# Hedgehog linear attention and softmax attention behind one gate: more score tiles on VectorE, feature sums and products on GpSimd, a written-out order

## The chip, the cores and the metric

The kernel runs on one core of a Trainium2 chip. The metric is device time in microseconds, the median of several runs. A core has five engines with a queue each: TensorE (PE, matrix products; PEld is its weight load), VectorE (DVE), ScalarE (ACT), GpSimd (POOL) and SyncE (SP, which here issues DMAs). They wait for one another by semaphores. TensorE writes to PSUM, 128 partitions by eight banks of 512 f32; here VectorE and ScalarE read PSUM, GpSimd works on SBUF alone.

## What is computed

One input `x` (1 x 2048 x 512, bf16) goes through two attention blocks of 32 heads with 16 features each, and a sigmoid gate mixes them:

```python
g = _sigmoid((x * gate_w).sum(-1, keepdims=True))
a = _A_ref(x, A_wqkv, A_w_phi, A_wo)      # linear attention, Hedgehog features
b = _B_ref(x, B_wqkv, B_wo)               # softmax attention
return g * a + (1 - g) * b
```

Block A maps q and k of each head by a 16 x 16 matrix, takes `softmax(p)` and `softmax(-p)` as 32 features, and computes `phi_q (phi_k^T v)` over `phi_q (sum of phi_k) + 1e-6`. Block B is plain softmax attention over 2048 keys: 32 heads x 2048 x 2048 exponentials. Both end in a 512 x 512 projection.

## The kernel before

**Block B** makes up most of the work. Its scores are cut into 32 blocks b of four heads i and 512 queries, each with 16 key tiles: 2048 tiles (b, i, kt) of 128 keys x 512 queries. A tile is one matmul with 32 rows of contraction (`qk_mm`, L1299 to L1303); four tiles of different heads can sit in the four row groups of the array. Values come by a second matmul into 32 columns (`pv_mm`, L1408 to L1415), accumulated in one bank, `psO`, for a whole block; a column of ones beside V gives the denominator.

The exponential of a tile is made in one of two ways:

- On **ScalarE**: a *slot* of two tiles in two PSUM banks, one `activation(Exp)` over 128 x 1024 (`add_exp`, L1392), into the ring `Ebuf`. Banks 0, 1 and 2, 3 alternate. 1304 tiles go this way, in 652 slots.
- On **VectorE**: `tensor_scalar` adds a constant and writes int16, whose bits read as bf16 are an approximate power of two (L1378; two tiles in one instruction, a *pair*, L1368). A *group* of up to four tiles of one block fills a buffer `t`. GpSimd then makes two copies shifted by constants with a 64-bit integer add (`shifted`, L1347 to L1358; L1354): `s` from `t`, then `m` over `s`. The value product is done for all three (`add_pvd`, L1416 to L1441): terms "t" and "s" in one piece of PE work, "m" in another, a round of up to four column tiles each. The counts of these tiles by block are `DN` (L31), 744 in all, in 195 groups. The scores of such a tile go to one of three shared banks, `MISC`, which also serve all other products. `PHASES` (L32) says which parts of SBUF serve as `t` and `s` from which block on.

When a block is done, `psO` is copied (L1507), the denominators go out to DRAM and come back transposed, are inverted, go out and come back broadcast as `Rb` (SP's moves in `add_norm`), and one product (L1523) scales two heads' rows into `oT`.

**Block A** is spread between as *fills* (`fill`, `drain`): a fill takes a bank, runs its matmuls, and a drain empties it. `columns` (L1060) splits a product with 128 output rows into four column tiles. For each 128 rows, `phi` (L1658) projects (L1062), takes exp of +p and -p on ScalarE (L1669), and for each two steps sums each head's 16 features. The sum is a product by the identity, 16 matmuls of 64 columns a step (L1676). For k, the reciprocal goes to `stat` (L1691) and scales V (`va_fill`, L1650; a small copy on GpSimd, L1655). For q, the ratio of the two sums (L1682, L1684, L1686) scales the second half of the features (`scaled_q`, L1703), and SP writes them to DRAM to be read transposed. `kv_half` and `kfinal` (L1732, L1735) build the masked state, `z_rest` and `q_rest` apply it.

**V** of block B for head rows 0 and 1 comes by `v_fill` (L1153), for rows 2 and 3 together by `v_pair` (L1166), 64 matmuls of 128 x 128 weights and 256 columns. `out_tile` and its kin do the projections; their sums meet in one bank.

**Order.** `Plan.add` notes each piece of work with engine, estimated duration, priority and what it reads and writes. `Plan.layout` (L538) lays all out in time on the five engines by a list schedule. It also puts in *fillers*: products with a zero weight tile (`zero_mm`, L1401 to L1406; L1403), where its estimate of TensorE's activity in the last 3.41 us (`WINDOW`, `ACTIVE`) falls under a limit, as pieces of their own ("idle") or ahead of a value product (`extra`). Pieces marked `lock` are kept from running on VectorE and GpSimd at once. `Plan.settle` (L780) then applies the table `MOVES`: changed places in each queue, pairs, `locks` (a GpSimd piece that waits for a given VectorE piece), banks, and fillers that are dropped. `Plan.emit` writes the queues; each engine runs its own strictly in that order, and waits where a piece needs another engine's.

Of the kernel before, what the change touches and what calls it, by code (L numbers as in the profile page):

```python
# [30 lines left out]
DN = (6, 20, 20, 24, 26, 26, 26, 20, 22, 22, 24, 18, 26, 24, 20, 26, 30, 22, 24, 26, 22, 24, 30, 26, 18, 22, 36, 18, 24, 24, 32, 16)  # L31
PHASES = ((0, ("x0", "x1", "pq", "o3", "y0"), ("y1", "pt", "woA", "woB", "o2")),  # L32
          (16, ("x0", "x1", "n0", "a0", "y0", "wk"), ("y1", "a1", "a2", "a3", "wv")),
          (27, ("x0", "x1", "n0", "a0", "y0", "wk"), ("y1", "a1", "a2", "a3", "wv", "wq")))
SIZES = (2, 2)
STICK = 58.273
# [39 lines left out]
ERING = 2 * EPAIRS  # L76
LAT, BANK_LAT = 0.12, 0.12
# [3 lines left out]
MOVES = {  # L81
# [9 lines left out]
    ),  # L91
    "act": (
# [3 lines left out]
    ),  # L96
# [337 lines left out]
    ),  # L434
}

# [1501 lines left out]
```

## Time and profile before

| | before |
|---|---|
| runs (us) | 676.28, 676.08, 675.73 |
| median | 676.08 |
| span of the profiled execution | 673.9 |
| TensorE busy | 665.2, 99% |
| ScalarE busy | 643.0, 95% |
| VectorE busy | 602.8, 89% |
| GpSimd busy | 401.0, 59% |
| DMA moved | 30.95 MB, mean 46 GB/s |

Busy time is that in which at least one instruction of the engine runs. Instructions that follow each other closely overlap in the records, so a group's busy time divided by its count is less than the mean duration of one. Groups are named by line, engine, output and input. The chain that ended last follows the program back from its last instruction, at each step to what released it.

### The profile page before, as it was taken

What the parts mean: (1) busy time and instruction counts of PE and PEld (TensorE: products, weight loads), DVE (VectorE), ACT (ScalarE), POOL (GpSimd) and SP (SyncE); (2) the same over time, 40 slices, a digit from 0 to 9 for tenths busy, and PEclk for the clock granted to TensorE, in tenths of its full rate; (3) what the DMA queues carried; (4) which work ended last, traced back from release to release, by engine and by line L of the source; (5) the groups of instructions that cost most, each with busy time, mean ns of one, the idle gap of its engine ahead of it and who ended that gap; (6) DMA issues with size and microseconds to landing.
All of it is one profiled execution on the core that took longest, in us unless ns stands there. A gap on an engine that the chain in (4) does not pass through costs nothing.

```text
span 673.9 us, 20931 instructions
## 1 busy us (share of the span) xinstructions
PE 665.2 (99%) x8995; PEld 233.7 (35%) x8995; DVE 602.8 (89%) x952; ACT 643.0 (95%) x723; POOL 401.0 (59%) x432
## 2 busy tenths in 40 slices
PE   8999999999999999999999999999999999999997
PEld 4332333434333333333333233323333233333333
DVE  4699889999998889999898989899999989999985
ACT  6999999999999999999999999999989998899995
POOL 7055557465666446565577676666865666555862
PEclk9999999999999999999999999999999999999999
DMA  7810101001010000000013032222311224032231
GB/s 129 157 40 12 32 13 26 11 11 23 7 27 11 11 21 8 19 17 15 21 41 102 26 67 62 54 44 64 77 54 41 63 77 105 18 89 66 66 72 40
DMA packets 67468, 30.95 MB, mean 46 GB/s; under 512 B 52696, under 2 KB 62296, under 8 KB 67376
## 3 DMA queue, kind: packets, MB, share of 16 engines
q1 hardware_dynamic: 66368, 28.95, 18.2%
q8 instruction: 70, 1.15, 0.7%
q10 hardware_dynamic: 576, 0.52, 0.2%
q0 software_dynamic: 432, 0.15, 0.2%
q14 instruction: 22, 0.18, 0.1%
HBM read 7.87 MB, written 8.88 MB: 25 GB/s over the span
## 4 chain that ended last, share of the span: by engine, by line
PE 81%; DVE 9%; ACT 7%; DMA 1%; issue 1%; SPq 0%; DVEq 0%
PE psS L1301 29%; PE psO L1413 28%; PE psS L1062 14%; ACT E_t L1392 6%; PE psS L1676 3%; DVE Tx_t L1378 2%; PE psO L1403 2%; DVE Ty_t L1378 1%; PE psS L1153 1%; PE psS L1166 1%; DVE WAT_t L1378 1%; DMA ld<-Tf_t 1%; PE psS L1773 1%; DMA Lq_t<-ld 1%; DVE vA_t L1378 1%
## 5 line engine op out<-in xcount | busy, mean ns | idle before, releaser
L1392 ACT ACTIVATE E_t<-psS 128x1024 bf16<-128x1024 f32 x652 | 611.6, 1049 | 20.0 <-PE psS L1301 16.1
L1301 PE MATMUL psS<-qz_t,kTB_t 32*128 32x512 bf16 x2048 | 272.9, 384 | 3.0 <-ACT E_t L1392 0.8
L1378 DVE TENSOR_SCALAR Tx_t<-psS 128x512 int16<-128x512 f32 x250 | 164.3, 681 | 13.2 <-PE psS L1301 11.8
L1301 PEld LDWEIGHTS psS<-qz_t,kTB_t 32*128 32x128 bf16 x2048 | 72.8, 91 | 231.5 <-ACT E_t L1392 100.7
L1413 PE MATMUL psO<-E_t,vaug_t 128*32 128x512 bf16 (+1 forms) x1304 | 106.4, 383 | 0.1
L1354 POOL INT64_ADD vA_t<-vA_t x72 | 71.5, 1001 | 35.7 <-PE psO L1413 21.3
L1378 DVE TENSOR_SCALAR Ty_t<-psS 128x512 int16<-128x512 f32 x110 | 73.7, 681 | 6.1 <-PE psS L1301 5.5
L1354 POOL INT64_ADD Ty_t<-Ty_t x42 | 43.3, 1032 | 15.0 <-PE psO L1413 10.2
L1413 PE MATMUL psO<-vA_t,vaug_t 128*32 128x512 bf16 (+1 forms) x520 | 49.9, 383 | 0.0
L1378 DVE TENSOR_SCALAR Tz_t<-psS 128x512 int16<-128x512 f32 x62 | 42.0, 685 | 3.3 <-PE psS L1301 2.2
L1413 PE MATMUL psO<-Ty_t,vaug_t 128*32 128x512 bf16 x436 | 43.9, 383 | 0.0
L1378 DVE TENSOR_SCALAR WAT_t<-psS 128x512 int16<-128x512 f32 x58 | 39.2, 685 | 4.2 <-PE psS L1301 3.8
L1354 POOL INT64_ADD phiQT_t<-Tx_t x19 | 18.1, 950 | 40.8 <-DVE Tx_t L1378 37.7
L1378 DVE TENSOR_SCALAR oT_t<-psS 128x512 int16<-128x512 f32 x56 | 37.4, 683 | 5.1 <-PE psS L1301 4.8
L1354 POOL INT64_ADD Ty_t<-Tx_t x29 | 29.7, 1025 | 20.4 <-DVE Tx_t L1378 12.1
L1413 PEld LDWEIGHTS psO<-E_t,vaug_t 128*32 128x32 bf16 (+1 forms) x1304 | 27.4, 95 | 35.3 <-issue 22.5
L1062 PE MATMUL psS<-Wp_t,xT_t 128*32 128x512 bf16 x512 | 37.7, 382 | 0.0
L1378 DVE TENSOR_SCALAR vA_t<-psS 128x512 int16<-128x512 f32 x52 | 35.1, 683 | 2.4 <-PE psS L1301 1.9
L1062 PE MATMUL psS<-xT_t,WB_t 128*32 128x512 bf16 x464 | 36.6, 383 | 0.0
L1354 POOL INT64_ADD vA_t<-Tx_t x22 | 22.0, 1002 | 21.5 <-DVE Tx_t L1378 17.5
L1378 DVE TENSOR_SCALAR Wp_t<-psS 128x512 int16<-128x512 f32 x48 | 31.9, 682 | 2.6 <-PE psS L1301 2.3
L1413 PE MATMUL psO<-Tx_t,vaug_t 128*32 128x512 bf16 x282 | 29.7, 387 | 0.0
(166 smaller groups left out, 914.4 us busy)
## 6 DMA issues: line engine op xcount, KB each, us to landing
dpq<-EA_t SPq DMA_DIRECT2D x16, 256.0 KB, 2.1
Rb_t<-lr SPq DMA_DIRECT2D x120, 32.0 KB, 1.8
dpo<-kv_t SPq DMA_DIRECT2D x16, 128.0 KB, 1.8
qz_t<-qz_t SPq DMA_DIRECT2D x120, 16.0 KB, 1.8
Tf_t<-Tf_t SPq DMA_DIRECT2D x60, 32.0 KB, 2.0
WB_t<-in_B_wqkv_dram SPq DMA_DIRECT2D x3, 384.0 KB, 4.3
out_dram<-WvA_t SPq DMA_DIRECT2D x8, 128.0 KB, 1.9
out_dram<-WB_t SPq DMA_DIRECT2D x6, 128.0 KB, 1.8
```

What stands on the lines that cost most here:

```text
L1062: ins = e.matmul(out[32 * i:32 * i + 32, :], lhsT=lhsT[:, 32 * i:32 * i + 32], rhs=rhs, start=start, stop=stop, tile_position=(0, 32 * i))
L1153: mms = [lambda e, ap, i=i, t=t: e.matmul(ap[:, 128 * i:128 * (i + 1)], lhsT=xT[:, t, NQ * c + 128 * i:NQ * c + 128 * (i + 1)], rhs=W_B[:, ...
L1166: mms = [lambda e, ap, i=i, t=t: e.matmul(ap[:, 256 * i:256 * (i + 1)], lhsT=xT[:, t, NQ * c + 128 * (2 * hf + i):NQ * c + 128 * (2 * hf + ...
L1301: return e.matmul(bank, lhsT=kT_B[32 * i:32 * i + 32, ROW[b // 2] % 2, 128 * kt:128 * (kt + 1)], rhs=qz[32 * i:32 * i + 32, b // 2 % 4, b ...
L1354: op = P.add("pool", P64 + W64 * size, d_prio(g["ts"][0]) - 5.0 + (0.0 if key == "s" else M_LATE), lambda e: e.int64_add(words(dst), words ...
L1378: ops.append(drain(f, mm, "dve", 0.70, d_prio(d), lambda e, ap, q=q: e.tensor_scalar(quarter(tb, q).bitcast(I16), ap, EXPB, 0.0, op0=ALU.a ...
L1392: op = P.add("act", EXP_OVH + 0.4267 * n, 0.0, lambda e: e.activation(Ebuf[:, j // 2 % EPAIRS, 512 * SZ[0] * (j % 2):512 * SZ[0] * (j % 2) ...
L1403: ins = e.matmul((psO if bank is None else bank)[32 * i:32 * i + 32, :], lhsT=zero[:], rhs=xT[:, 0, 0:NQ], start=bank is not None, stop=ba ...
L1413: return e.matmul(psO[32 * i:32 * i + w, :], lhsT=vaug[:, kt, o:o + w], rhs=rhs, start=start, stop=stop, tile_position=(0, 32 * i), skip_g ...
L1676: mms = [lambda e, ap, n=n, f=f: e.matmul(ap[:, 64 * n:64 * n + 64].rearrange("p (s g j) -> p s g j", s=2, j=4), lhsT=ident[:], rhs=es[n][ ...
L1773: mms = [lambda e, ap, g=g: e.matmul(ap[:, 64 * g:64 * g + 64], lhsT=qT(g)[:, 128 * j:128 * (j + 1)], rhs=kzbd[:, g, 0:64], start=True, st ...
```

## The change

- `DN` rises by two in 17 blocks: 778 tiles on VectorE, 1270 on ScalarE (635 slots). Pairs fall from 54 to 34. Groups stay 195; those of two tiles become groups of four in these blocks.
- `Tz`, a `t` buffer, goes. From block 2 to 15 the two halves of `WAT` (`n0`, `n1`) serve as `t` beside `x0`, `x1`, `o3`, `y0`.
- The feature sums: in place of the product by the identity, four adds on GpSimd for each step of 128 rows, from 16 features to 8, 4, 2, 1 (512, 256, 128 and 64 results, f32). They use `quart` and `half`, the latter over the weights `Wbd` and `Wbp` once these have been used.
- Products of two SBUF inputs move from VectorE to GpSimd: the ratio (8), the scaling of the features (16), the scaling by `Rb` (15), the two masks (`kfinal`). The copy L1684 goes. The reciprocals stay on VectorE and read SBUF in place of PSUM.
- `v_pair` uses `columns`: 256 matmuls of 32 output rows.
- The planner (`layout`, `mates`, `choose`, `settle`) goes. `place` reads the order of every queue from `TABLE` (list positions of the pieces), the banks from "homes" and the pairs. The queues have 260 (SP), 677 (ACT), 2590 (PE), 957 (DVE) and 597 (POOL) entries. The list for `extra` is empty, and no entry of PE's is a filler. There is no list of locks.
- `WIDE` would allow slots of three tiles; it is empty, so `add_qk`, `add_exp` and `add_pv` do as before, with `Ebuf` addressed by `E_AT`.

```diff
-DN = (6, 20, 20, 24, 26, 26, 26, 20, 22, 22, 24, 18, 26, 24, 20, 26, 30, 22, 24, 26, 22, 24, 30, 26, 18, 22, 36, 18, 24, 24, 32, 16)
-PHASES = ((0, ("x0", "x1", "pq", "o3", "y0"), ("y1", "pt", "woA", "woB", "o2")),
+DN = (6, 20, 20, 24, 28, 28, 28, 20, 24, 24, 24, 20, 28, 24, 20, 28, 32, 24, 24, 28, 24, 24, 32, 28, 20, 24, 36, 20, 24, 24, 32, 16)
+PHASES = ((0, ("x0", "x1", "o3", "y0"), ("y1", "pt", "woA", "woB", "o2")),
+          (2, ("x0", "x1", "n0", "o3", "n1", "y0"), ("y1", "pt", "woA", "woB", "o2")),
           (16, ("x0", "x1", "n0", "a0", "y0", "wk"), ("y1", "a1", "a2", "a3", "wv")),
...
+    def place(self, table):
+        self.closed = {b: list(b.last) for b in self.every}
+        for b in self.every:
+            b.first = b.free
+        homes = {7 if b.index is None else b.index: b for b in self.every}
+        known, bank = list(self.ops), iter(table["homes"])
+        for k, n in table["extra"]:
+            known[k].extra = n
+        self.order = {e: [known[k] if k >= 0 else self.filler(k) for k in table[e]] for e in ENGINES}
+        for op in self.order["pe"]:
+            if op.acq is not None:
+                op.acq.bank = homes[int(next(bank))]
+            op.banks = op.take if op.take is not None else [op.acq.bank] if op.acq is not None else []
+        for a, k in table["pairs"]:
+            self.join(known[a], known[k])
...
-    Wbd = sb([128, KT, 128], name="Wbd")
-    Wbp = sb([128, KT, 128], name="Wbp")
+    Wbs = sb([128, 2, KT, 128], name="Wbs")
+    Wbd, Wbp = Wbs[:, 0], Wbs[:, 1]
+    half = Wbs[:].rearrange("p a t c -> p (a t c)").bitcast(F32)
...
+    quart = sb([128, 256], F32, name="quart")
...
     def v_pair(c, hf, prio):
-        mms = [lambda e, ap, i=i, t=t: e.matmul(
-            ap[:, 256 * i:256 * (i + 1)], lhsT=xT[:, t, NQ * c + 128 * (2 * hf + i):NQ * c + 128 * (2 * hf + i + 1)],
-            rhs=W_B[:, t, 2 * D + 256:3 * D], start=(t == 0), stop=(t == KT - 1)) for i in range(2) for t in range(KT)]
+        mms = [lambda e, ap, i=i, t=t: columns(
+            e, ap[:, 256 * i:256 * (i + 1)], xT[:, t, NQ * c + 128 * (2 * hf + i):NQ * c + 128 * (2 * hf + i + 1)],
+            W_B[:, t, 2 * D + 256:3 * D], t == 0, t == KT - 1) for i in range(2) for t in range(KT)]
...
-                P.add("dve", 0.7, -40, lambda e: e.tensor_tensor(oT[:, r, qc, :], Tf[:, 0, :], Rb[:], ALU.mult),
-                      reads=[("Tf", 0), "Rb"], writes=[("oT", qc, r)], name=f"T2.{b}").lock = True
-                P.ops[-1].pad = T2_PAD
+                P.add("pool", 1.25, -40, lambda e: e.tensor_tensor(oT[:, r, qc, :], Tf[:, 0, :], Rb[:], ALU.mult),
+                      reads=[("Tf", 0), "Rb"], writes=[("oT", qc, r)], name=f"T2.{b}")
...
-        mms = [lambda e, ap, n=n, f=f: e.matmul(ap[:, 64 * n:64 * n + 64].rearrange("p (s g j) -> p s g j", s=2, j=4), lhsT=ident[:],
-                                                rhs=es[n][0].rearrange("p (g s f j) -> p f s g j", s=2, f=DH, j=4)[:, f],
-                                                start=(f == 0), stop=(f == DH - 1)) for n in range(2) for f in range(DH)]
-        f, mm = fill(S_PRIO + prio, mms, [k for _, k in es] + ["ident"], name=f"S{qk}.{st}", chunk=8, dur=0.042, cols=64)
+        pair = stat[:] if qk else statq[:, st % 8 - 1:st % 8 + 1, :]
+        pkey = [("rs", 0), ("rs", 1)] if qk else [("sq", st % 8 - 1), ("sq", st % 8)]
+        for n, (e_ap, ek) in enumerate(es):
+            src, k = e_ap.rearrange("p (h f j) -> p h f j", f=DH, j=4), DH
+            while k > 1:
+                k //= 2
+                if k > 1:
+                    to = (quart if k == 4 else half)[:, 0:64 * k].rearrange("p (h f j) -> p h f j", f=k, j=4)
+                    u, v = src[:, :, 0:k, :], src[:, :, k:2 * k, :]
+                else:
+                    to = pair[:, n, :].rearrange("p (s g j) -> p g s j", s=2, j=4)
+                    u, v = [src[:, :, x, :].rearrange("p (g s) j -> p g s j", s=2) for x in (0, 1)]
+                P.add("pool", 0.1 + 0.14 * k, prio, lambda e, to=to, u=u, v=v: e.tensor_tensor(to, u, v, ALU.add), reads=[ek if k == 8 else "quart" if k == 2 else "half"],
+                      writes=["half" if k in (8, 2) else "quart"] if k > 1 else [pkey[n]], after=wp_mms if k == 8 else (), name=f"h{qk}.{st - 1 + n}.{k}")
+                src = to
         if qk == 0:
...
+            P.add("dve", 0.55, prio, lambda e: e.reciprocal(ratio[:], pair[:, :, 32:64]), reads=[("sq", st % 8 - 1), ("sq", st % 8)],
+                  writes=["ratio"], name=f"rs{qk}.{st}")
+            P.add("pool", 0.25, prio, lambda e: e.tensor_tensor(ratio[:], ratio[:], pair[:, :, 0:32], ALU.mult),
+                  reads=["ratio", ("sq", st % 8 - 1), ("sq", st % 8)], writes=["ratio"], name=f"rt{qk}.{st}")
...
-        P.add("dve", 0.7, prio, lambda e: e.tensor_tensor(minus, minus, by, ALU.mult),
-              reads=["ratio", ("EA", b)], writes=[("EA", b)], name=f"phi0.{st}.1").lock = True
+        P.add("pool", 1.25, prio, lambda e: e.tensor_tensor(minus, minus, by, ALU.mult),
+              reads=["ratio", ("EA", b)], writes=[("EA", b)], name=f"phi0.{st}.1")
...
-    P.layout()
...
-    P.settle(MOVES)
+    P.place(TABLE)
```

More of the change, by code (lines that the diff above doesn't have):

```diff
@@ L35 @@
 SIZES = (2, 2)
+WIDE, WIDE_SPAN = (), (8, 540)
 STICK = 58.273
@@ L76 @@
 ERING = 2 * EPAIRS
+E_AT = [sum(1024 + 512 * (k in WIDE) for k in range(r)) for r in range(ERING + 1)]
 LAT, BANK_LAT = 0.12, 0.12
@@ L523, in join_writes @@
         self.readers[key] = []
-    def mates(self, a, b):
-        return PAIRING and b.kind == "D1" and a.half[0] == b.half[0] and abs(a.rel.bank.index - b.rel.bank.index) == 1 and (
-            a.half[1] - b.half[1]) * (a.rel.bank.index - b.rel.bank.index) > 0
-    def choose(self, op, banks):
-        def key(b):
-            cross = op.half is not None and any((b.index - k) * (op.half[1] - q) < 0 for k, q in self.filled.get(op.half[0], {}).values())
-            return cross, max([0.0] + [x.end for x in b.last])
-        best = min(banks, key=key)
-        if op.half is not None:
-            self.filled.setdefault(op.half[0], {})[op.half[1]] = (best.index, op.half[1])
-        return best
@@ L768, in join, with filler @@
+    def filler(self, kind):
+        op = Op("pe", 0.215, 0.0, None, "idle")
+        op.deps, op.kind = list(self.ground), "zero"
+        if kind == -3:
+            op.acq = op.rel = Fill(self.misc)
+            op.fn = lambda e: self.idle(e, op.acq.bank.ap)
+        else:
+            op.fn = self.idle if kind == -1 else self.idle_o
+        self.ops.append(op)
+        return op
     def join(self, op, other):
@@ L770, in join @@
         b, b2 = op.rel.bank.index, other.rel.bank.index
-        assert other.half[0] == n_g and abs(b - b2) == 1 and (q - q2) * (b - b2) > 0
+        assert other.half[0] == n_g and (q - q2) * (b - b2) > 0
         op.fn = lambda e, a=(min(q, q2), max(q, q2)), b=(min(b, b2), max(b, b2)): wide(e, a, b)
@@ L1006, in _build @@
                   name="wob", lat=5.0)]
-    warm = P.add("dve", 0.3, -10, lambda e: e.memset(Ebuf[:, 0, 0:512], 0.0), writes=[("E", 0)], name="wz")
+    warm = P.add("dve", 0.3, -10, lambda e: e.memset(Ebuf[:, 0:512], 0.0), writes=[("E", 0)], name="wz")
     def warm_fn(e):
@@ L1229, in _build @@
     cur, rot = 0, 0
+    is_wide = lambda j: j % ERING in WIDE and WIDE_SPAN[0] <= j < WIDE_SPAN[1]
     def next_tile():
@@ L1245, in _build @@
         j = len(slots)
-        act = [t for t in (next_tile() for _ in range(SZ[j % 2])) if t is not None]
+        act = [t for t in (next_tile() for _ in range(SZ[j % 2] + is_wide(j))) if t is not None]
         if not act:
@@ L1271, in _build @@
     bufs["wq"] = (Wp[:, :, 0:D], p_ops[0])
-    for k in range(1):
+    for k in range(2):
         bufs[f"n{k}"] = (flat(WAT[:, 4 * k:4 * k + 4, :]), wp_ops)
@@ L1320, in add_qk @@
         op.full = 0.21
-        op.kind, op.heads = "qk", [t[1] for t in ts]
+        op.kind, op.heads = "qk", [t[1] for t in ts[:2]]
+        if len(ts) == 3:
+            third[j] = fill(-99, [lambda e, ap: qk_mm(e, ts[2], ap)], reads, [bS[lowS]], name=f"q3.{j}", after=exp_ops[j - 2:j - 1])
+            third[j][1].kind, third[j][1].heads = "q3", [ts[2][1]]
         op.lat += QK_PAD
@@ L1329, in add_qk @@
         return op
-    made, dq_ops, last_d1 = [0], [], []
+    made, dq_ops, last_d1, third = [0], [], [], {}
     holder = {}
@@ L1392, in add_exp @@
         op = P.add("act", EXP_OVH + 0.4267 * n, 0.0, lambda e: e.activation(
-            Ebuf[:, j // 2 % EPAIRS, 512 * SZ[0] * (j % 2):512 * SZ[0] * (j % 2) + 512 * n], psS[:, 512 * base:512 * (base + n)], ACTF.Exp, scale=ESCALE),
-            reads=[("S", j % 2)], writes=[("E", j % ERING)], name=f"exp{j}")
+            Ebuf[:, E_AT[j % ERING]:E_AT[j % ERING] + 512 * n], psS[:, 512 * base:512 * (base + n)], ACTF.Exp, scale=ESCALE),
+            reads=[("S", j % 2)], writes=[("E", j % ERING)], after=[third[j][1]] if j in third else [], name=f"exp{j}")
+        if j in third:
+            op.rel = third[j][0]
         op.kind, op.extra = "exp", j % 2
@@ L1480, in add_pv @@
                        writes=["psO"] if first else (),
-                       after=pv_last[-1:] + (block_pvd.get(b, []) if last else []), name=f"pv{j}")
+                       after=pv_last[-1:] + (block_pvd.get(b, []) if last else []), name=f"pv{j}.{b}")
             op.full = 0.215 * rounds
@@ L1899, in _build @@
     P.add("sp", 0.1, 1e6, lambda e: None, reads=[("out", i) for i in range(NT)], name="end")
-    P.layout()
-    q = P.order["pe"]
-    P.order["pe"] = [o for o, nxt in zip(q, q[1:] + [None]) if not (
-        o.name == "idle" and o.acq is None and nxt is not None and nxt.kind == "qk" and len(nxt.heads) == 3)]
-    P.settle(MOVES)
+    P.place(TABLE)
     sems = {e: sem("s_" + e) for e in ENGINES}
```

318 lines of the change are left out of this document (34 added, 284 removed), and 570 rows, old and new, of tables (MOVES, TABLE).

## The prediction, made before the result was known

> **What bounds the kernel now.** I read the busy table first, then the chain that ended last, then ScalarE's waits, then busy time by stage. The profiled execution spans 673.9 us; the median of the three runs is 676.08 us, so 2.2 us lie outside the span. I work in the span and add the 2.2 at the end.
>
> ```profile
> span 673.9 us, 20931 instructions
> PE 665.2 (99%) x8995; PEld 233.7 (35%) x8995; DVE 602.8 (89%) x952; ACT 643.0 (95%) x723; POOL 401.0 (59%) x432
> PE 81%; DVE 9%; ACT 7%; DMA 1%; issue 1%; SPq 0%; DVEq 0%
> ```
>
> Two engines look full, PE at 99% and ACT at 95%. The chain decides between them: 81% of it is PE, 7% ACT. The chain by line, with a decimal, and what ACT waited for (us in total, times, longest):
>
> ```profile
> by line: PE psS L1301 28.5%; PE psO L1413 28.1%; PE psS L1062 14.2%; ACT E_t L1392 6.4%; PE psS L1676 2.6%; DVE Tx_t L1378 2.2%; PE psO L1403 2.2%; DVE Ty_t L1378 1.2%; PE psS L1153 1.1%; PE psS L1166 1.0%; DVE WAT_t L1378 0.8%; issue 0.7%;
> ACT E_t L1392 <- PE psS L1301: 16.1, 42, 1.1
> ACT E_t L1392 <- PE psO L1413: 2.4, 2, 1.9
> ```
>
> So ACT is the second wall: its exponentials wait 18.5 us in all, always for PE. By stage (columns PE, PEld, DVE, ACT, POOL; clock; DMA):
>
> ```profile
> 0.00:17.00 17.00, 14.70 (x145) 7.06 (x145) 7.30 (x27) 11.26 (x14) 12.39 (x26) 1.00 0.71 131
> 17.00:650.00 633.00, 629.98 (x8551) 219.05 (x8553) 580.80 (x901) 614.65 (x692) 380.29 (x399) 1.00 0.18 43
> 650.00:674.00 24.00, 20.49 (x309) 7.55 (x301) 14.73 (x25) 17.11 (x19) 8.27 (x8) 0.99 0.23 56
> ```
>
> The long middle has PE at 99.5%, ACT at 97.1% (614.65/633), DVE at 91.8% (580.80/633), POOL at 60%. A change that frees PE alone soon hits ACT; this one frees both, and loads POOL.
>
> **ScalarE.** 34 tiles leave it, two to an exponential: 17 fewer at L1392.
>
> ```profile
> L1392 ACT ACTIVATE E_t<-psS 128x1024 bf16<-128x1024 f32 x652 | 611.6, 1049 | 20.0 <-PE psS L1301 16.1 <-PE psO L1413 2.4
> ```
>
> One lasts 1049 ns but overlaps the next, so the price is 611.6/652 = 0.938 us. 17 x 0.938 = 15.9 us. With ACT's idle time as it is, the span becomes 673.9 - 15.9 = 658.0; with all 18.5 us of waits for PE gone as well, 639.5.
>
> **TensorE.** The rows, in order: scores, values of ScalarE's tiles, V of two head rows, and four rounds of a product in column tiles (from the timeline).
>
> ```profile
> L1301 PE MATMUL psS<-qz_t,kTB_t 32*128 32x512 bf16 x2048 | 272.9, 384 | 3.0 <-ACT E_t L1392 0.8 <-DVE Tx_t L1368 0.7 <-DVE vaug_t L1173 0.2
> L1413 PE MATMUL psO<-E_t,vaug_t 128*32 128x512 bf16 (+1 forms) x1304 | 106.4, 383 | 0.1
> L1166 PE MATMUL psS<-WB_t,xT_t 128*128 128x256 bf16 x64 | 9.2, 275 | 0.0
> 123.19 1.05 PE L1062 MATMUL psS<-xT_t,WB_t 128*32 128x512 bf16 x16
> ```
>
> The feature sums (512 small products) leave PE: 2.6% of the chain, 17.5 us. The fillers leave: 2.2%, 14.8 us. They stand where PE had nothing ready, so this term may be worth nothing: its ends are 0 and 14.8, and what replaces it is then plain idle time. The 17 score rounds: L1301 has 28.5% of the chain, 192 us over 652 slots, 0.295 each, 5.0 us. The value products of 34 E tiles: 34 x 106.4/1304 = 2.8 us. Together 40.1.
>
> Added: 34 single scores for VectorE, between 0 (beside a pair on other rows) and 272.9/2048 = 0.133 each, 4.5 us; I take 2. The value terms of D tiles need no new rounds: the tiles of the blocks sum to 744 and 778, but in groups of up to four both make 195 groups; 17 groups of two become four. Their 102 extra products run in columns that stood empty, 0 to 102 x 0.082 (the E-tile price) = 8.3 us; I take 2. V in column tiles: 64 rounds of four products of 256 columns. A 512-column round costs 1.05/4 = 0.26 us, so 64 rounds cost 8.4 (half of it) to 16.8 against 9.2 now: -0.8 to +7.6; I take 0. Sum: -36 us, bounds -40.9 to -5 (every added term at its upper end, the fillers worth nothing). PE alone would allow 638, in the worst case 669, so only if all goes wrong is PE still first.
>
> **VectorE.** Single evictions 636 to 710, pairs 54 to 34 (778 = 710 + 2 x 34).
>
> ```profile
> 0.00:674.00 674.00, 407.15 (x636) 1.00 0.19 46
> 0.00:674.00 674.00, 65.75 (x54) 1.00 0.19 46
> L1703 DVE TENSOR_TENSOR EA_t<-EA_t,ratio_t 128x512 bf16<-128x512 bf16 x16 | 10.8, 682 | 0.0
> L1523 DVE TENSOR_TENSOR oT_t<-Tf_t,Rb_t 128x512 bf16<-128x512 f32 x15 | 10.2, 682 | 0.0
> L1686 DVE TENSOR_TENSOR ratio_t<-ratio_t,statq_t 128x64 f32<-128x64 f32 x8 | 1.7, 209 | 0.0
> L1684 DVE COPY statq_t<-psS 128x64 f32<-128x64 f32 x8 | 1.3, 168 | 0.0
> L1732 DVE TENSOR_TENSOR kzbd_t<-kv_t,mask_t 128x512 bf16<-128x512 f32 x1 | 0.7, 686 | 0.0
> ```
>
> The first two rows are L1378 (one tile, 0.640 us) and L1368 (a pair, 1.218). +74 x 0.640 - 20 x 1.218 = +23.0. Gone: 10.8 + 10.2 + 1.7 + 1.3 + 0.7 = 24.7. Net -1.7: the same work in a shorter span, 579/617 = 93.8% of the middle instead of 91.8%.
>
> **GpSimd** takes all of that and the sums. Per step of 128 rows four adds of 512, 256, 128 and 64 results, 32 steps; 31 products of 512; 8 of 64; the mask products of 512 and 32. No two-input operation runs on POOL in this trace. Nearest rows:
>
> ```profile
> L1050 POOL COPY Wbp_t<-Wbd_t 128x512 bf16<-128x512 bf16 x1 | 1.1, 1081 | 3.5 <-DMA Wbd_t<-in_A_w_phi_dram 3.5
> L1655 POOL CAST vA_t<-stat_t 128x64 bf16<-128x64 f32 x16 | 3.7, 241 | 5.6 <-DVE stat_t L1691 5.1 <-DVE gT_t L1624 0.5
> 33.23 0.61 POOL L1354 INT64_ADD phiQT_t<-Tx_t  x1 [15.18 <-DVE Tx_t L1378]
> 33.82 1.03 POOL L1354 INT64_ADD Ty_t<-Tx_t  x1
> ```
>
> The two copies give 1.875 ns an element on 0.12 us. At that price a step costs 1.08 + 0.60 + 0.36 + 0.24 = 2.28 us, 32 steps 73, the products 31 x 1.08 + 8 x 0.24 + 1.3 = 36.7: 110 us, the lower end. At twice the slope (two operands read in turn) a step costs 4.08, the sum is 199 us, the upper end. I take 110, for on VectorE the rows with two inputs (682 ns) cost what the one-input tile eviction costs, so a second operand need not show. The 17 groups that grow from two to four tiles make 34 adds longer by 1.03 - 0.61 = 0.42: 14 us more. POOL: 401 + 14 + 110 = 525 us, 80% of 658; with 199, 614 or 93%.
>
> The Trainium skill, GPSIMD Engine Reference, section 4.1 (Engine selection), advises against this move: two-input elementwise work is about twice as slow there as on VectorE. Its figure in section 3.1, 4497 ns for an add of 2048, makes an estimate of 125 us in place of 110 for POOL, which moves no bound here; no run shows it yet.
>
> **Waits.** A sum waits for the feature exponential; behind it in POOL's queue stand the shifts of later groups, and for those PE's value terms:
>
> ```profile
> PEld psO L1413 <- POOL vA_t L1354: 4.0, 16, 0.4
> L1676 PE MATMUL psS<-phiK_t,ident_t x256: 189/191/203, 85.1 to 270.3; 128*128 128x64 bf16 x128
> L1676 PE MATMUL psS<-EA_t,ident_t x256: 189/191/203, 336.8 to 596.6; 128*128 128x64 bf16 x128
> Rb_t<-lr SPq DMA_DIRECT2D x120, 32.0 KB, 1.8
> ```
>
> PE hardly waits for POOL today (longest 0.4 us). The eight pair sums of each kind are some 26 and 37 us apart, room for 4.6 us of adds. The product by Rb, now on POOL, waits for a transfer of 1.8 us: at worst 15 x 1.8 = 27 us of POOL's idle time, hidden while POOL has 100 and more. SP's row writes come behind POOL's products instead of VectorE's, later by about 0.5 us each; the steps' spacing hides that. If the covers fail, PE, whose order is fixed, stands, and so does all else.
>
> **Sum.** ACT sets the end: 658.0 less the part of its 18.5 us of waits that goes. PE gains 36 - 16 = 20 us of slack, which speaks for much; VectorE is at 93.8%, which speaks against. I take a quarter, 4.6: 653.4, plus 2.2: **655.6 us**. The bounds of this case are 641.7 (all waits gone) and 660.2 (none), to which I add some microseconds for late POOL results: 646 to 662 holds most of it.
>
> **Rivals.** (1) VectorE becomes the bound. At its present 91.8% its 579 us need 631, plus the 41 of both ends: 672 + 2.2 = 674; at 96% they need 603, which is under ACT. For it: only three spare PSUM banks feed it. Against: its idle time today ends on PE's scores. Between the two, 662 to 674, say 667: 0.14. In the other direction, under 646, if more than three quarters of ACT's waits vanish: 0.04.
>
> (2) Slower: POOL becomes the bound. Its first shift is at 33 us, its last work about 10 us before the end, so it has some 630 us. POOL's 380 of the middle and 8 of the end, with the 14 of the longer shifts, leave 228 for products, sums and waits. From there on it decides: with 199 us of new work, more than 29 us of waits that nothing fills make it so. Its idle time before shifts, from the view of L1354:
>
> ```profile
>   PE psO L1413: 101.2, 71
> ```
>
> If half of this, 51 us, stays, 199 + 51 - 228 = 22 us stand over: 676 + 22 = 698. Against it: it needs the upper end. 0.09.
>
> (3) Slower: the clock. Without fillers PE rests more.
>
> ```profile
> L1013 PE MATMUL psS<-E_t x7: 609/634/634, 1.2 to 3.7; 128*128 128x512 bf16 x7
> L1301 PE MATMUL psS<-qz_t,kTB_t x2048: 371/384/386, 7.8 to 664.9; 32*128 32x512 bf16 x187
> 200.00:250.00 50.00, 0.00 (x0) 0.00 (x0) 1.00 0.06 13
> 122.10 0.39 PE L1413 MATMUL psO<-Tx_t,vaug_t 128*32 128x512 bf16 x4
> 122.31 0.39 PE L1413 MATMUL psO<-Ty_t,vaug_t 128*32 128x512 bf16 x4
> ```
>
> The seven warm-up products follow each other in 0.42 us (2.5/6), later rounds in 0.21: half pace exists, although the clock column reads 1.00 then too. After 7.8 us no score product takes over 386 ns, not even from 200 to 250 us, where no filler runs (third row). A microsecond at half pace costs half a microsecond of PE; with 36 us of relief against today it makes the kernel slower from 72 us of it on; 100 us make 638 + 50 + 2 = 690. 0.08. The Trainium skill, TensorE: Matmul & The Clock Gate, Part 1, has the clock halve after an idle window of about 3.4 us; by that nothing happens here, as no gap of that length is in sight; the trace agrees as far as it shows.
>
> (4) The new order holds as many waits as the work it saves, and nothing changes, 676: 0.03.
>
> **Chances.** Forecast 0.62, under 646 0.04, VectorE 0.14, POOL 0.09, clock 0.08, no change 0.03. Faster by over 0.2% (what a measurement can tell) 0.80, within 0.03, slower 0.17. Leaving out 0.04 below and about 0.16 above, the range is 646 to 674.
>
> **What would show it.** L1392 635 times near 0.94 us and ACT's share of the middle over 97.5%; the chain moved from PE to ACT and DVE; PE under 97% busy and no product of 32 rows over 390 ns after 8 us; DVE busy 601; POOL busy 525, a 512-add near 1.1 us; PE's waits for POOL still short. I am wrong if POOL is above 600 or PE's share of the chain stays at 80%.

## The result, and the profile after

The changed kernel takes **2114.24 us** (median of 4 runs, 2109.09 to 2117.59), the kernel before 675.93 us beside it (675.73 to 676.28). The ratio is 3.125, 95% interval 3.119 to 3.130. The forecast was 655.6 us. Medians and ranges here are of all executions, while the ratios leave out the few that ran in a slower state (one of six without fillers, one of four with the rows on GpSimd), so a quotient of two medians can differ from the ratio beside it.

The page of the changed kernel: span, busy time, the clock row, and the chain by engine.

```profile
span 2107.3 us, 20454 instructions
PE 856.0 (41%) x8443; PEld 224.7 (11%) x8443; DVE 617.8 (29%) x957; ACT 651.6 (31%) x706; POOL 537.3 (25%) x601
...
PEclk9867666857555577555556555556555556556678
...
issue 59%; PE 19%; POOL 15%; DVE 3%; ACT 3%; DMA 0%; POOLq 0%; DVEq 0%; SPq 0%
```

No engine is busy for half the span, and no engine leads the chain: 59% of it is "issue", time in which the engine at that place waited for nothing that the profile shows. Before, "issue" was 1% and PE 81%. The clock, 9 (90% or more) in nearly every slice before, is down to 5 or 6.

What the engines waited for (us in total, times, longest):

```profile
ACT E_t L1070 <- PE psS L976: 1414.0, 260, 50.3
...
PEld psO L1093 <- POOL vA_t L1032: 370.2, 42, 39.7
...
POOL Wbs_t L1368 <- issue: 254.9, 36, 7.8
...
POOL vA_t L1032 <- issue: 228.2, 38, 6.6
...
DVE ratio_t L1372 <- POOL statq_t L1368: 168.4, 8, 45.4
```

ScalarE waits for scores of PE, PE for the shifts of GpSimd, VectorE for its sums; and GpSimd's own rows say "issue", always with a longest wait of 6 to 8 us. So the queue to read is GpSimd's. Its rows from 81 us on, where the first two-input operation stands (start, duration, operation; in brackets the idle time ahead of it):

```profile
81.73 1.26 POOL L1203 TENSOR_TENSOR oT_t<-Tf_t,Rb_t 128x512 bf16<-128x512 f32 x1 [7.58 <-issue]
82.95 0.23 POOL L728 COPY mask_t<-mask_t 128x64 bf16<-128x64 bf16 x1
89.06 1.03 POOL L1032 INT64_ADD Ty_t<-Ty_t  x1 [5.89 <-issue]
97.32 1.14 POOL L1368 TENSOR_TENSOR Wbs_t<-phiK_t 128x512 f32<-128x512 bf16 x1 [7.23 <-issue]
98.54 0.73 POOL L1368 TENSOR_TENSOR quart_t<-Wbs_t 128x256 f32<-128x256 f32 x1
99.35 0.45 POOL L1368 TENSOR_TENSOR Wbs_t<-quart_t 128x128 f32<-128x128 f32 x1
99.88 0.32 POOL L1368 TENSOR_TENSOR stat_t<-Wbs_t 128x64 f32<-128x64 f32 x1
...
108.23 1.03 POOL L1032 INT64_ADD phiQT_t<-Tx_t  x1 [5.93 <-issue]
```

Read the brackets. Each time the kind of operation changes from INT64_ADD to TENSOR_TENSOR, some 7 us pass; each time it changes back, some 6. Between operations of one kind nothing passes. The copy at 82.95 starts without a pause, and the 5.89 us behind it are the change from the product before the copy to the shift behind it. Over GpSimd's whole timeline there are 111 changes to TENSOR_TENSOR (median 7.11 us, 6.69 to 7.79, together 791.9) and 111 back (median 5.98, 5.70 to 6.63, together 664.6): **222 changes, 1456.5 us**. GpSimd's busy 537.3, these 1456.5 and some 113 of other idle time make its span of 2107.3.

GpSimd's queue also names what stands in each pause. These rows are from the view of a source line; a MODIFY_POOL_CONFIG is not counted as busy, lasts for 1 to 20 ns and so is in no table of busy time (first the changed kernel from 70 to 90 us, then the kernel before from 0 to 40 us; count, shortest, median and longest duration in ns, first and last start in us):

```profile
L1203 POOLq MODIFY_POOL_CONFIG  x2: 11/11/11, 74.1 to 74.1; - x2
L1354 POOLq MODIFY_POOL_CONFIG  x2: 12/12/12, 18.1 to 18.1; - x2
```

In the changed kernel two such rows start at 74.1 us, and the product behind them at 81.73; two more start at 83.4, and the shift behind them at 89.06. There are 446 in all: two for each of the 222 changes, and two ahead of the first shift. The kernel before has these first two alone.

By stage (PE, PEld, DVE, ACT, POOL; clock):

```profile
0.00:50.00 50.00, 46.75 (x476) 18.67 (x476) 35.24 (x72) 44.02 (x50) 24.35 (x37) 1.00 0.54 110
50.00:100.00 50.00, 32.81 (x405) 9.64 (x401) 29.42 (x48) 34.44 (x40) 18.22 (x20) 0.88 0.08 18
100.00:500.00 400.00, 183.27 (x1934) 49.21 (x1934) 136.85 (x206) 143.85 (x160) 119.51 (x139) 0.68 0.02 5
```

In the first 50 us, before any change of kind, the clock is 1.00 and PE 94% busy. The first pause starts at 74 us.

The rows that answer to those of before: the exponentials, the scores, and four groups on GpSimd that are new.

```profile
L1070 ACT ACTIVATE E_t<-psS 128x1024 bf16<-128x1024 f32 x635 | 617.9, 1047 | 1423.2 <-PE psS L976 1414.0
L976 PE MATMUL psS<-qz_t,kTB_t 32*128 32x512 bf16 x2048 | 343.5, 480 | 62.1 <-DVE WAT_t L1056 24.1
```

```profile
L1368 POOL TENSOR_TENSOR quart_t<-Wbs_t 128x256 f32<-128x256 f32 x32 | 23.2, 725 | 137.1 <-issue 136.1
L1203 POOL TENSOR_TENSOR oT_t<-Tf_t,Rb_t 128x512 bf16<-128x512 f32 x15 | 18.8, 1253 | 79.3 <-issue 79.3
L1368 POOL TENSOR_TENSOR Wbs_t<-phiK_t 128x512 f32<-128x512 bf16 x16 | 18.3, 1146 | 78.8 <-issue 42.5 <-ACT E_t L1070 35.7
L1390 POOL TENSOR_TENSOR EA_t<-EA_t,ratio_t 128x512 bf16<-128x512 bf16 x16 | 16.7, 1048 | 86.5 <-issue 86.3
```

The two-input operations themselves are as cheap as hoped; the number behind the bar, idle just before the group, is the one that matters. The 35.7 put down to ACT L1070 stand before first adds of a step too, in pieces of up to 7.6 us, and are counted among the 222: they are of the same length.

The theories: **A**, GpSimd pays 6 to 7 us for each change between INT64_ADD and TENSOR_TENSOR, and nothing else went wrong. **B**, the clock falls because the fillers are gone. **C**, the written order holds waits of its own. **D**, two-input work on GpSimd is slow, or collides with VectorE.

### The profile page after: what moved, and what is told of

Same layout as the page of the kernel before. It is cut to its first block, busy times and chain, and to the rows that moved or that the text cites. A ratio compares the mean times of both kernels' runs of the same rounds, so it can differ in the third digit from the quotient of the medians.

```text
span 2107.3 us, 20454 instructions
## 1 busy us (share of the span) xinstructions
PE 856.0 (41%) x8443; PEld 224.7 (11%) x8443; DVE 617.8 (29%) x957; ACT 651.6 (31%) x706; POOL 537.3 (25%) x601
## 4 chain that ended last, share of the span: by engine, by line
issue 59%; PE 19%; POOL 15%; DVE 3%; ACT 3%; DMA 0%; POOLq 0%; DVEq 0%; SPq 0%
PE psO L1093 8%; PE psS L976 7%; POOL vA_t L1032 3%; PE psS L735 3%; ACT E_t L1070 3%; POOL Wbs_t L1368 2%; POOL Ty_t L1032 2%; POOL WB_t L1032 1%; POOL quart_t L1368 1%; POOL WoA_t L1032 1%; POOL phiQT_t L1032 1%; POOL oT_t L1032 1%; POOL WoB_t L1032 1%; DVE Tx_t L1056 1%; POOL EA_t L1390 1%
## 5 line engine op out<-in xcount | busy, mean ns | idle before, releaser
L1070 ACT ACTIVATE E_t<-psS 128x1024 bf16<-128x1024 f32 x635 | 617.9, 1047 | 1423.2 <-PE psS L976 1414.0
L976 PE MATMUL psS<-qz_t,kTB_t 32*128 32x512 bf16 x2048 | 343.5, 480 | 62.1 <-DVE WAT_t L1056 24.1
L1056 DVE TENSOR_SCALAR WAT_t<-psS 128x512 int16<-128x512 f32 x170 | 114.3, 684 | 255.1 <-PE psS L976 254.3
L1093 PE MATMUL psO<-E_t,vaug_t 128*32 128x512 bf16 (+1 forms) x1270 | 139.7, 480 | 25.0 <-DVE Tf_t L1187 25.0
L1093 PE MATMUL psO<-vA_t,vaug_t 128*32 128x512 bf16 (+1 forms) x548 | 71.4, 535 | 156.6 <-POOL vA_t L1032 146.7
L1093 PE MATMUL psO<-Ty_t,vaug_t 128*32 128x512 bf16 x440 | 57.0, 520 | 189.2 <-POOL Ty_t L1032 72.2
L1093 PE MATMUL psO<-WAT_t,vaug_t 128*32 128x512 bf16 (+1 forms) x180 | 23.2, 501 | 142.0 <-POOL vA_t L1032 58.3
L1368 POOL TENSOR_TENSOR quart_t<-Wbs_t 128x256 f32<-128x256 f32 x32 | 23.2, 725 | 137.1 <-issue 136.1
L1093 PE MATMUL psO<-WB_t,vaug_t 128*32 128x512 bf16 (+1 forms) x152 | 19.7, 508 | 85.8 <-POOL WB_t L1032 85.8
L1093 PE MATMUL psO<-WoB_t,vaug_t 128*32 128x512 bf16 x144 | 18.7, 504 | 79.6 <-POOL WoB_t L1032 79.6
L735 PE MATMUL psS<-xT_t,WB_t 128*32 128x512 bf16 x480 | 49.1, 484 | 0.0
```

The lines of the kernel that those rows point to most:

```text
L735: ins = e.matmul(out[32 * i:32 * i + 32, :], lhsT=lhsT[:, 32 * i:32 * i + 32], rhs=rhs, start=start, stop=stop, tile_position=(0, 32 * i))
L976: return e.matmul(bank, lhsT=kT_B[32 * i:32 * i + 32, ROW[b // 2] % 2, 128 * kt:128 * (kt + 1)], rhs=qz[32 * i:32 * i + 32, b // 2 % 4, b ...
L1056: ops.append(drain(f, mm, "dve", 0.70, d_prio(d), lambda e, ap, q=q: e.tensor_scalar(quarter(tb, q).bitcast(I16), ap, EXPB, 0.0, op0=ALU.a ...
L1070: op = P.add("act", EXP_OVH + 0.4267 * n, 0.0, lambda e: e.activation(Ebuf[:, E_AT[j % ERING]:E_AT[j % ERING] + 512 * n], psS[:, 512 * bas ...
L1093: return e.matmul(psO[32 * i:32 * i + w, :], lhsT=vaug[:, kt, o:o + w], rhs=rhs, start=start, stop=stop, tile_position=(0, 32 * i), skip_g ...
L1368: P.add("pool", 0.1 + 0.14 * k, prio, lambda e, to=to, u=u, v=v: e.tensor_tensor(to, u, v, ALU.add), reads=[ek if k == 8 else "quart" if k ...
```

## The experiments

Spans and busy times are of the profiled runs; times are medians, each ratio is to the kernel before on the same chip.

**The price by itself.** GpSimd alone in a bare kernel.

```diff
+run(*[i64] * 6)
+run(*[i64, tt] * 8)
+run(*[tt] * 6)
+run(*[tt, ts] * 4)
+run(*[i64, ts] * 4)
+run(*[i64, cp] * 6)
+run(*[i64, ms] * 4)
+run(*[tt, cp] * 4)
+run(*[i64, lambda: tt(64)] * 4)
```

> A bare kernel: GpSimd alone runs a fixed list of operations, each waiting for the one before; it leaves out the whole computation of the reference and writes zeros. The list: 6 INT64_ADD (128x1024 bf16 as 64-bit words); 8 pairs of INT64_ADD and a 512-wide TENSOR_TENSOR; 6 TENSOR_TENSOR; 4 pairs of TENSOR_TENSOR and one-input TENSOR_SCALAR; 4 pairs of INT64_ADD and TENSOR_SCALAR; 6 pairs of INT64_ADD and copy; 4 pairs of INT64_ADD and memset; 4 pairs of TENSOR_TENSOR and copy; 4 pairs of INT64_ADD and a 64-wide TENSOR_TENSOR. Theory A (GpSimd pays for every change between INT64_ADD and TENSOR_TENSOR): an idle of about 7 us ahead of each TENSOR_TENSOR that follows an INT64_ADD and about 6 us ahead of each INT64_ADD that follows a TENSOR_TENSOR, at 64 columns as at 512, whatever else the core does; no idle above 0.3 us in the runs of one kind, nor with copies and memsets. The changed kernel does not show TENSOR_SCALAR, so the pairs with it tell which group it belongs to. Theory B (the PE clock without fillers), C (the written order waits on its own) and D (two-input operations are slow, or share a port with VectorE): no idle above 0.5 us anywhere in this kernel, since PE, the order and VectorE are absent; by D the TENSOR_TENSOR itself would be well under the 1.14 us of the changed kernel.

Measured: 308.17 us, span 306.3. From GpSimd's timeline:

```profile
43.57 1.03 POOL L23 INT64_ADD shifted<-ones  x1 [5.79 <-issue]
51.37 1.25 POOL L26 TENSOR_TENSOR fsum<-fa,fb 128x512 f32<-128x512 f32 x1 [6.77 <-issue]
...
128.09 10.63 POOL L26 TENSOR_TENSOR fsum<-fa,fb 128x512 f32<-128x512 f32 x8 [7.18 <-issue]
138.81 1.54 POOL L29 TENSOR_SCALAR scaled<-fa 128x512 f32<-128x512 f32 x1
...
162.97 1.53 POOL L29 TENSOR_SCALAR scaled<-fa 128x512 f32<-128x512 f32 x1 [7.00 <-issue]
...
217.84 0.61 POOL L32 CAST copied<-fb 128x512 bf16<-128x512 f32 x1
218.55 1.04 POOL L23 INT64_ADD shifted<-ones  x1
...
228.69 0.53 POOL L35 MEMSET cleared<- 128x512 bf16 x1
...
277.49 0.31 POOL L26 TENSOR_TENSOR fsum<-fa,fb 128x64 f32<-128x64 f32 x1 [6.89 <-issue]
```

With all other engines silent the price is the same: 6.75 to 7.72 us toward TENSOR_TENSOR, 5.68 to 6.02 back, at 64 columns as at 512. TENSOR_SCALAR goes with TENSOR_TENSOR (no idle between them, 7.0 after an INT64_ADD); the copy with change of type (CAST) goes with both, and memset with INT64_ADD. That rules out contention as the source of the pauses, and no other engine is needed for them. The rows of MODIFY_POOL_CONFIG, for shift, add and TENSOR_SCALAR:

```profile
L23 POOLq MODIFY_POOL_CONFIG  x34: 1/1/11, 1.0 to 291.9; - x34
L26 POOLq MODIFY_POOL_CONFIG  x26: 1/1/11, 14.5 to 298.7; - x26
L29 POOLq MODIFY_POOL_CONFIG  x8: 1/1/1, 156.0 to 202.3; - x8
```

These are 68: two for each of the 33 changes and two ahead of the first shift. The lines of the copy and the memset have none.

**The change without changes of kind, first way.** The shifts as memsets.

```diff
-            return ap[:, 0:size, :].bitcast(I64)
+            return ap[:, 0:size, :].bitcast(F32)
...
-lambda e: e.int64_add(words(dst), words(src), step * 0x0001000100010001)
+lambda e: e.memset(words(dst), 0.0)
```

> The changed kernel with its 380 or so INT64_ADD shifts as memsets of the same bytes, in the same places of the same queues, with the same waits; it leaves out the shift of the score tiles on VectorE (the copy is set to zero), so their weights differ. A memset of 1536 bf16 columns took 1.39 us before, of 512 0.54 us, so one of 1024 words is put at about 0.9 us, near the 1.03 us of the shift, and the copies and memsets of the changed kernel stand without idle beside both kinds. Theory A: no change of kind is left, POOL is busy for some 500 to 560 us, its idle labelled issue falls from 1456 us to under 20, and the time falls to 650 to 760 us, about 690. Theory B (clock): all products stay at their measured 856 us of PE time and the time at 860 us or above, the clock row at 5 to 6. Theory C (order): the queues are the same, so the time stays near 2114 us. Theory D (two-input work): the two-input operations are unchanged, so above 1500 us.

Measured: 665.39 us (663.32 to 668.30), ratio 0.985 (0.982 to 0.988). Busy times and clock row of its page:

```profile
PE 646.5 (97%) x8443; PEld 214.1 (32%) x8443; DVE 599.3 (90%) x957; ACT 626.1 (94%) x706; POOL 491.2 (74%) x601
...
PEclk9999999999999999999999999999999999999799
```

The order is the same on every queue, there are no fillers, all 169 two-input operations are in: 1449 us are gone. B, C and D fall as causes of the loss. GpSimd's busy time came out under the 500 to 560 us that were expected.

**Second way.** The shifts as they are, each two-input operation of GpSimd as a copy of one input.

```diff
-lambda e, to=to, u=u, v=v: e.tensor_tensor(to, u, v, ALU.add)
+lambda e, to=to, u=u, v=v: e.tensor_copy(to, u)
... and so at the ratio, the scaling, the rows by Rb and the two masks
```

> The mirror of the run with memsets: the changed kernel with the INT64_ADD shifts as they are, and each of the 169 two-input operations of GpSimd as a copy of one of its inputs, in the same place with the same waits; it leaves out the feature sums' additions, the scaling by the ratio, the division of the rows and the masks. Copies took 1.08 us (512 bf16) and 0.61 us (512 f32 to bf16) with no idle beside either kind. Theory A: no change of kind is left, idle labelled issue under 20 us, POOL busy 500 to 560 us, 655 to 685 us, about 667, like the run with memsets. Theory D (the two-input work itself is the cost) also expects a short time here; but it expected the run with memsets to stay long, which had all the two-input work. Theory C (order): near 2114 us.

Measured: 662.98 us (661.78 to 663.63), ratio 0.980 (0.978 to 0.982).

```profile
span 661.1 us, 20010 instructions
PE 646.0 (98%) x8443; PEld 214.2 (32%) x8443; DVE 600.1 (91%) x957; ACT 626.2 (95%) x706; POOL 479.0 (72%) x601
...
PE 68%; ACT 17%; DVE 7%; DMA 4%; SPq 3%; issue 1%; DVEq 0%
```

Neither INT64_ADD nor TENSOR_TENSOR is slow in this program; only both in one queue are. Both this run and the last have 2 rows of MODIFY_POOL_CONFIG, as the kernel before. They show about what the change would be worth without the price: 10 to 13 us less than before, with 58 and 46 us less work on GpSimd than the changed kernel has.

**The same operations, fewer changes.** GpSimd's list in the table in another order: operations of one kind stand together as far as their inputs allow, 34 changes in place of 222.

```diff
 "pool": (
-    the 597 entries as they stand
+    the same 597 entries, regrouped by kind
```

> The changed kernel with GpSimd's queue alone in another order: operations of one kind stand together as long as their inputs allow it, so that there are 34 changes between INT64_ADD and TENSOR_TENSOR in place of 222; not one operation is added, removed or moved to another engine. Theory A: 34 x 6.55 = 223 us of idle in place of 1456; POOL's own sum is 537 + 223 + some 80 = 840 us, and since the other engines keep their order and now wait for operations that stand later than before, 840 to 1150 us, about 1000. Theory B (clock), D (two-input work): the same work at the same place of PE, near 2114 us. Theory C (order): a queue made without regard to time can only wait longer, 2114 us or more.

Measured: 1017.79 us (1014.75 to 1021.60), ratio 1.508 (1.505 to 1.512).

```profile
PE 723.2 (71%) x8443; PEld 217.2 (21%) x8443; DVE 606.9 (60%) x957; ACT 637.5 (63%) x706; POOL 538.6 (53%) x601
```

GpSimd is as busy as in the changed kernel (538.6 against 537.3). Its timeline has 34 changes, 120.6 + 102.1 = 222.7 us, 6.55 each, and 70 rows of MODIFY_POOL_CONFIG. Against the 661.1 of the copies the span is longer by 352: 223 is the size of the changes. The other 129 were not taken apart; that they are waits for what the regrouping put late, with a clock of 0.81 on the mean, is likely and not shown.

**The two-input operations on VectorE.**

```diff
-P.add("pool", 0.1 + 0.14 * k, prio, lambda e, to=to, u=u, v=v: e.tensor_tensor(...
+P.add("dve", 0.1 + 0.14 * k, prio, lambda e, to=to, u=u, v=v: e.tensor_tensor(...
... and so at the ratio, the scaling, the rows by Rb and the two masks
```

> The changed kernel with all 169 two-input operations of GpSimd (128 sums, 8 ratio products, 16 scalings, 15 row products, the two masks of KV) on VectorE, put into its queue where an untimed merge by due time puts them; everything else in the same order, the shifts still INT64_ADD. Theory A: no change of kind is left on GpSimd; POOL busy about 400 us, idle labelled issue under 20 us; VectorE carries its 618 us plus 45 to 90 us, 663 to 708, and becomes the engine nearest to its limit: 690 to 780 us, about 725. The clock row goes back above 9 for most of the span, although there are no fillers. Theory B (clock): 5 to 6 in the clock row and 860 us or more. Theory C (order): the order of PE, ACT and SP is the same, so above 1500 us. Theory D agrees with A here on the direction.

Measured: 744.79 us (739.73 to 746.45), ratio 1.101 (1.097 to 1.105).

```profile
PE 682.7 (92%) x8443; PEld 215.5 (29%) x8443; DVE 684.9 (92%) x1126; ACT 640.4 (86%) x706; POOL 428.3 (58%) x432
```

No TENSOR_TENSOR on GpSimd, no long idle. VectorE, 84.8 us fuller than with the copies, now has the largest share of the chain, 45% against PE's 41%. As a cure for the changed kernel it takes away two thirds of its time, but it loses to before by a tenth.

**A few changes of kind in the kernel before.** The 15 products by Rb alone go to GpSimd.

```diff
+        late = [o for o in self.order["dve"] if o.name.startswith("T2.") and int(o.name[3:]) < 30]
+        for op in late:
+            self.order["dve"].remove(op)
+            op.eng = "pool"
+            ... into GpSimd's list ahead of the shift that starts next
```

> The kernel before with the 15 products of rows by Rb alone moved from VectorE to GpSimd, between its INT64_ADDs; nothing else changed. GpSimd's work grows by 15 x 1.25 = 19 us, and it stood idle for 273 us. Theory A: 30 changes of kind at 7.1 and 6.0 us, 197 us more on GpSimd, 617 us in all, less than the span. Were only GpSimd's sum to count, nothing would be seen, about 676. But each change is one piece of 13 to 14 us in front of shifts that TensorE waits for in its fixed order, and the shifts ran with little lead, so part of each piece reaches the end: between 700 and 870 us, about 820, with clock 0.9 or above. Theory D (the work itself): 19 us are hidden in the idle time, 670 to 680 us. Theory B: the fillers are in, 676 us.

Measured: 852.13 us (847.08 to 860.18), ratio 1.258 (1.255 to 1.261). The product's idle time, who waits for it, and who waits for that:

```profile
POOL oT_t L1535 <- issue: 100.7, 14, 7.6
...
DVE Tf_t L1519 <- POOL oT_t L1535: 53.8, 9, 8.0
...
PE psO L1425 <- DVE Tf_t L1519: 49.7, 9, 7.6
```

The 30 changes take 107.5 + 87.8 = 195.3 us, the span grows by 849.3 - 673.9 = 175.4. GpSimd is busy for 419.7 of 849.3 and yet holds up the rest: its spare time of 273 us hid only a tenth of the changes. The rows show two ways. The late product keeps `Tf`, so VectorE's copy of `psO` is late, and with it PE's next block (49.7 us at L1425). And the shifts behind the piece of 14 us are late: PE's products wait 39 us for them. The loss is not a matter of the sum of GpSimd's work. The clock, expected at 0.9 or above, was 0.89.

**The other parts of the change, one at a time on the kernel before.** Fillers out:

```diff
+        for op in self.order["pe"]:
+            if op.kind != "exp":
+                op.extra = 0
+        self.order["pe"] = [o for o in self.order["pe"] if o.name != "idle"]
```

> The kernel before without its fillers (all 75 or so rounds of products with the zero tile that only keep TensorE busy, and those ahead of value products), the order of everything else untouched. Theory A (the price of changing kind on GpSimd is all that went wrong): the clock stays as it was, since the changed kernel with memsets for shifts ran without fillers at a mean clock of 0.995; the time is between 661 us (all 14.8 us of the chain come back) and 676 us (they stood where nothing was ready), about 672. Theory B (without fillers the clock falls): products of 32 rows above 390 ns on the mean and 690 us or more.

Measured: 685.83 us (679.53 to 690.25), ratio 1.011 (1.008 to 1.015): slower, by neither theory's number. From 8 to 30 us it shows

```profile
8.00:30.00 22.00, 20.29 (x160) 7.24 (x158) 5.63 (x11) 16.76 (x17) 6.37 (x13) 0.63 0.72 145
```

where before showed

```profile
8.00:30.00 22.00, 21.49 (x265) 8.51 (x261) 10.04 (x17) 21.74 (x24) 6.36 (x13) 1.00 0.82 145
```

The clock is 0.63, although PE looks 92% busy. Of the 265 products 39 are fillers, so of its own PE does 160 against 226 in the same time. By stretches of 2 us the clock is 1.00 up to 12 us and 0.50 from 14 to 30. The pauses of PE from 9.7 to 12.8 us, just before, are of 0.53 us each, between pairs of score products. So the fillers do hold up the clock, at the start. To see whether the later ones do so too, six of the 75 came back:

```diff
+            if op.kind != "exp" and op.end > 30.0:
+                op.extra = 0
+        self.order["pe"] = [o for o in self.order["pe"] if o.name != "idle" or o.end <= 30.0]
```

> The kernel before with the first six of its 75 filler rounds (those of the planner's first 30 us) and without the other 69, order of everything else untouched. With none at all it took 685.83 us and its clock from 8 to 30 us was 0.63, against 1.00 before. If the fillers are worth their place only there, the clock of that stretch comes back to 1.00 and the time to 676 us or a little under, 668 to 678, about 674. If the later ones hold the clock up as well, it stays above 680 us, with score products above 388 ns on the mean.

Measured: 676.09 us (675.04 to 680.33), ratio 1.001 (0.999 to 1.002). From 8 to 30 us the clock is 1.00 again. The other 69 fillers are worth nothing, for or against: removing them saves no time. V in column tiles:

```diff
-        mms = [lambda e, ap, i=i, t=t: e.matmul(
+        mms = [lambda e, ap, i=i, t=t: columns(
```

> The kernel before with the V products of two head rows in column tiles alone (64 products of 128 columns wide become 256 of 32), order untouched. The prediction's bounds for this part are -0.8 to +7.6 us of TensorE, taken as 0: so 675 to 684 us, about 676. Theory B (column tiles with 256 columns lower the clock or run at half pace): 8 us longer or more, 684 up. Theory A says nothing else of it: GpSimd is not touched.

Measured: 675.11 us (674.72 to 676.74), ratio 0.999 (0.998 to 1.000): no difference that this measurement can tell. And both, no fillers and V in columns:

> The kernel before without fillers and with V in column tiles. If the two parts do not touch one another, their two differences add up: with 672 and 676 for the parts, about 672, and between 661 and 684. Theory B: slower than either.

Measured: 685.60 us (684.10 to 687.81), ratio 1.014 (1.012 to 1.016). It lies above the expected 661 to 684, which took 672 for the run without fillers. It is that run again: V in columns neither adds nor hides anything.

## Why the prediction was wrong

**The step that failed** is the sum for GpSimd, 401 + 14 + 110 = 525 us, with the waits behind it. It priced 169 operations by their duration and put nothing between them, so the price of a change between two kinds of operation stood at 0 without a reason. The work was right: POOL 525 us forecast, 537.3 measured; the two-input rows 110 forecast, 123.4 measured (near the 125 that the estimate from the Trainium skill, GPSIMD Engine Reference, section 3.1, gave). The room was wrong: "room for 4.6 us of adds" holds for the adds, not for the 13 us of a change there and back. 222 changes at 6.56 us are 1456 us; the changed kernel's span less that of the kernel with copies is 2107.3 - 661.1 = 1446.

Could it have been seen? The trace of before holds no TENSOR_TENSOR on GpSimd, and its INT64_ADDs stand among copies and casts, which costs nothing in these runs either. It does hold one pair of MODIFY_POOL_CONFIG, at 18.1 us, ahead of the first shift; no pause shows there, since that shift waits for VectorE until 33.2. The Trainium skill, GPSIMD Engine Reference, section 2.1 (Instruction dispatch), says that the first call to a freshly loaded kernel (there, a routine of GpSimd's own cores) pays a load of about 6 us "with no visible profile instruction", measured from the row MODIFY_POOL_CONFIG on; the prediction cited the page for the price of a two-input operation and passed over this. The trace agrees: that row stands at the head of the pauses, two at each change, and the 5.98 and 7.11 us are near its size. So the pauses read as such a load, paid again at each change. The load itself has no row here; what is shown is the price per change, between which operations, and the row that stands before it.

**Bounds now, ScalarE.** Right. Without the price 17 exponentials fewer give, in the kernel with copies,

```profile
L1070 ACT ACTIVATE E_t<-psS 128x1024 bf16<-128x1024 f32 x635 | 595.5, 1081 | 23.4 <-PE psS L976 21.3 <-PE psO L1093 0.2
L976 PE MATMUL psS<-qz_t,kTB_t 32*128 32x512 bf16 x2048 | 281.7, 385 | 6.5 <-DVE Ty_t L1056 1.7 <-ACT E_t L1070 1.4 <-DVE Wp_t L1046 0.9
```

611.6 to 595.5, so 16.1 for a forecast of 15.9.

**The sum, beside the price.** Its 653.4 took a quarter of ScalarE's 18.5 us of waits as gone. Idle time before the exponentials grew instead, from 20.0 to 23.4: 673.9 - 16.1 + 3.4 = 661.2, and the span is 661.1. The waits of the exponentials for PE rose from 18.5 to 21.5. So 8 us of the forecast were wrong even without the changes of kind.

**TensorE.** Mis-sized, and the likely reason for those 8 us: -36 forecast, 665.2 to 646.0 = -19.2 in busy time, and the chain stayed with PE (68%). The filler term, taken at 14.8, is worth nothing (69 of 75 gone, ratio 1.001), as its own lower end said. Without it the forecast relief of PE is 21 us, only 5 more than that of ScalarE, so "only if all goes wrong is PE still first" was too sure. The scores were to fall by 5.0 and rise by 2; the group went from 272.9 to 281.7. How much of that is the unpaired scores for VectorE was not tried by itself. V at 0 was right (ratio 0.999).

**VectorE.** Right: -1.7 forecast, 602.8 to 600.1.

**The rivals.** That GpSimd becomes the bound, at 0.09, named the engine and not the mechanism: it asked for more than 228 us of work and waits, and priced itself by slow two-input work. With 199 us of such work it would have been a loss of 22. The clock did fall, to a mean of 0.63, but as a result: PE stands for up to 50 us at a time, and GpSimd's own time already fills the span. Alone the missing fillers cost 1.1% in the old order, and there the rival's "no gap of that length is in sight" was no guard: the clock halved with pauses of 0.53 us in sight. In the new order the clock is 0.997 on the mean without them (the kernel with copies), and 1.00 from 8 to 30 us; what makes that difference is not shown. VectorE as the bound came true only where the products were given to it.

**The signs of being wrong.** "POOL above 600" could not have caught it: POOL is busy 537.3. A limit on busy time does not see time between operations. Nor did PE's share of the chain stay at 80%; it fell to 19%. What did catch it is "PE's waits for POOL still short": the longest was 0.4 us before and is 50.6 after.

No kernel here beats both: those at 663 and 665 us leave work out, VectorE has no room (745), regrouping keeps 34 changes (1018), and GpSimd cannot take even the 15 products (852).

## What to carry to other kernels

Before an engine gets a kind of operation that it has not run in the trace, ask what it costs to change to it and back, count the changes in the order as written, and multiply; one short bare kernel with both kinds in turn gives the price. A stretch labelled "issue" with one and the same length again and again, on one engine, at each change of operation, is such a price; the rows of that engine's queue, read by source line, can name what stands in it (here MODIFY_POOL_CONFIG). Spare time on an engine hides work only in pieces smaller than the lead of those who wait for it: 15 pieces of 14 us cost 175 us on an engine that was idle for 273.

## What the runs showed of the hardware

- GpSimd, in the changed kernel and in the bare one: 5.7 to 6.6 us from TENSOR_TENSOR to INT64_ADD, 6.7 to 7.8 us the other way, at 64 columns as at 512, with the other engines at work or silent; TENSOR_SCALAR counts as TENSOR_TENSOR; copy, cast and memset are free beside both.
- Two rows of MODIFY_POOL_CONFIG stand at each of these changes (446 rows for 222 changes, 70 for 34, 68 for 33, 62 for 30, each with two for the first shift; 2 in every kernel without changes).
- A two-input add on GpSimd (512 bf16 to f32) took 1.15 us; on VectorE, in the run with the operations there, 0.75 to 0.94.
- PE can be 92% busy in the busy table and do 160 of its own products where it did 226, at a clock of 0.63; the busy share alone does not show a lower clock.
- Without fillers the clock fell to 0.50 for 16 us after some 3 us with pauses of 0.53 us between pairs of products.
